# A gated recurrence with a low-rank mixer: transposes moved to ScalarE's DMA queue, one batch's input to the MLP formed as sums, and a new instruction order

## The chip, the cores and the metric

The kernel runs on one core of one Trainium2 chip. A core has a matmul engine (TensorE, PE), a vector engine (VectorE, DVE), an activation engine (ScalarE, ACT), a general engine (GpSimd, POOL) and a queue engine (SyncE, SP) that here only issues DMA transfers. The metric is device time in microseconds. The profile's span runs from the first to the last instruction of one profiled execution and is about 2 us shorter than the time.

## The reference

There are four batches of 768 tokens, eight heads of 48 channels (384 channels in all). First comes a linear recurrence with a gate per channel, then a low-rank mixing of tokens with a residual, then a two-layer MLP with a residual.

```python
for t in range(S):                                  # per batch and head
    state = alpha[t][:, None] * state + outer(k[t], v[t])
    y[t] = q[t] @ state
x = y                                               # (batch, 768, 384)
u = x + (x.T @ U @ V).T                             # U: 768x32, V: 32x768
out = u + relu(u @ w_ch1) @ w_ch2                   # 384 -> 1536 -> 384
```

## The kernel before, in words

**Tiles.** Tokens are cut into chunks of 128. Batches 0 and 1 (`PAIR`) are handled two tokens per partition and four heads at a time by `stage_pair`, batches 2 and 3 by `stage_gla`, one chunk and all eight heads at a time. Both do the same things: the logarithm of alpha on ACT (`lt`), one cumulative-sum matmul group on PE (`cb`, in `f_cum`), and three exponentials of it on ACT: `ai` (with minus), `aa`, and `tot`, the decay over a whole chunk. Then rk = k times ai and rq = q times aa on POOL or DVE; these two are transposed to kT and qT; scores are matmuls of kT with qT (`sc`), masked on DVE into `pm`; the state is carried from chunk to chunk by `db`, `sm` and `st`; and y comes from `pm`, rv (v in bf16) and the old state, and is copied into `xb`.

**The totals.** Two heads lie side by side on the 128 partitions, and the state needs their decays separately, with exact zeros for the other head. In `f_cum` a matmul of the identity with `offd` (8 columns holding 0 or -30000) is added to the sums, so that one exponential gives both the values and the zeros.

**The transposes.** A transpose is either a PE matmul group against the identity (L435 for pairs, L604 for `stage_gla`), whose result ACT or DVE copies out of PSUM, or a DMA transpose from SBUF to SBUF. The set `TRD` names the chunks whose kT and qT come by DMA: of batch 3, chunks 2 to 5. `TRU` names the batch, 3, whose u is transposed by DMA. Before, SyncE's queue issues them all (L595 and L735).

**The mixer.** `stage_mix` forms utx, the 32-row product of U and x. For a batch in `XT` (0 and 1) the transposed u is made on PE in one go: x is multiplied by the identity (L718) and the mixer's product is added to the same PSUM tile (L721); u itself is never formed, so `mlp2` adds the mixer's part once more at its end (L803). For the other batches the mixer's product (L730) is added to x on DVE, giving `ub`, and that is transposed, by PE (L746) for batch 2 or by DMA for batch 3.

**The MLP.** `mlp1` is 12 column groups by two halves of the tokens, three matmuls of 128x384 each (L773), whose results ACT or DVE pass through a maximum with zero into `h1t` (L783, L785). `mlp2` is 12 matmuls of 128x384 for each chunk (L798), then the residual add on DVE (L807) and the store (L808).

**The order.** Nothing runs in the order of the source. Each step is registered in `Plan` with its possible engines and a cost in nanoseconds. `TABLE` lists the steps' numbers in the order in which they are emitted, with a letter where the engine is chosen (A for ACT, V for DVE, G for POOL). `place` walks the table, picks buffers and keeps a clock for each engine; the clocks decide which buffer of a pool a step gets and how many dummy matmuls (`filler`) keep PE busy in the first 28 us. [...]

**Waits of transfers.** Every transfer, whichever queue issues it, takes one of eight semaphores in turn. It is issued only after the one that had the same semaphore, eight transfers earlier, has landed.

Of the kernel before, what the change touches and what calls it, by code (L numbers as in the profile page):

```python
# [8 lines left out]
FP32 = mybir.dt.float32  # L9
BF16 = mybir.dt.bfloat16  # L10
# [29 lines left out]
class Plan:  # L40
# [3 lines left out]
    BEGIN = {"DVE": 4400.0, "POOL": 3300.0, "ACT": 2900.0}  # L44
# [43 lines left out]
    def place(self, table):  # L88
# [6 lines left out]
        end = {}  # L95
        for x in table.split():
# [15 lines left out]
            if eng == "DVE" and op.port:  # L112
                t = max(t, port - self.PORT)
            op.t = t
            if eng == "SP" and op.mode == "X":
                dma = max(dma, t) + cost
                clock[eng] = t + cost
                end[op] = dma + 850.0
            elif eng == "SP":
                dma = max(dma, t + 600.0) + cost  # L120
                clock[eng] = max(t + 450.0, dma - 3500.0)
                end[op] = dma + 2000.0
            else:
                if eng == "PE" and op.mode != mode:
                    cost += self.SWITCH
                    mode = op.mode
                clock[eng] = end[op] = t + cost
                if eng == "POOL" or (eng == "DVE" and op.port):
                    port = end[op]
            for b in op.bufs:  # L130
                b.left -= 1
                b.last = max(b.last, end[op] + self.LAT[eng])
                if b.left == 0:
                    b.pool.free[b.idx] = b.last
# [19 lines left out]
67 65 69 179 61 182 201 184 157 77 62 63 183 66 204 160 205 187G 247 189 161 162 207 64 68 191V 164V 166 186V 188 190A 185 168V 165V 73 71 167 192 70  # L154
181G 180G 224 206 163 159G 169V 81 74 170 194 172 193 75 158G 209G 3 78 79 76 82 72 195 250 227 196 208V 83 173 211 210 251 228 268 229 197 213A 2 231G
171 174 80 271 175 198 212V 214 273 274 272 84 85 176 89 232V 233 253 252 234 215 254G 6 5 199 177 255G 4 226G 275G 203G 15 31 33 35 236V 23 13 17 93
19 21 27 29 235A 237 43 25 87 86 1 97 39 90 216 200A 238 256 257 230 225A 259A 258V 240 202A 178A 241 239 242 260 277 276V 243 244 217 249G 218 270G
219 88 95 278 37 41 262 261 51 47 49 91 279A 245 220 280A 222 248A 94 269G 8 281 7 57 59 45 55 221 388 263 283 53 101 96 32 34 16 36 264 18 14 24 20 92
284 285 98 105 391 410 394 246A 107 103 99 100 102 265 266 413 392 393 22 28 30 26 286 282 287 9 11 395G 0 267V 223V 288A 289 290 295 10V 12A 291A 414
292 304 298 299 293 296 300A 396G 301 417G 302 305 297A 307 308 294V 306V 303V 309A 415 332 330 328 352 354 331A 329A 432 416 336 355V 353A 435 356 438  # L160
357A 333V 344 312 340 320 314 345A 315A 313A 436 346 310 338 342 321V 455 337V 437 109 106 343V 112 104 108 113 316 398 334 318 347V 341V 335V 339V
311A 44A 40A 400A 390A 440G 38G 42G 348 458 397 419 326 322 317V 323V 349V 399A 327A 401 319A 461 389G 460 459 403 418V 421V 48G 439G 383 404 358 442
324 325A 50A 402 405 406 368 46G 420 350 412G 52A 444A 58A 441 411G 434G 433G 462G 407G 351V 422V 443A 363 364 359 56A 54A 60A 478 423 445 384 369 370
424 446 425 481 360 499 482 483 426 448 486G 447 361 371 449 502 385 365 505 450V 504 453 507G 427 386 428 366 509 464 488 485G 429G 511V 463V 110 362
111 129 367 457A 503 456A 490A 454A 408 471 378 409A 619 466A 451 506V 465 430 487 508 117 379 133 467V 472 123 116 121 114 118 115 473G 468 119 120
122 489V 130 125 431A 484 510A 479A 480A 500A 131 127 124 387 136 474 135 126 128 137 149 491 512 470 452V 493 492 469 373 494 380 475G 501A 638 621
374 495 640 515 623 622 496G 513 516 514 476 625 517V 375 497 627 381 629V 477A 626 620 642 641 376 718 498A 624 518 628 630V 720 519A 529 520 521 631
722 721 723 658 522V 535 523 526 633 833 527 538 539 524 530 528A 525V 660 536 532 533 531A 537V 634 662 540A 661 663 545 561 551 635 534V 587 559 644
664 645 639 585 588V 560A 581 546A 557 541 659 562A 643 569 567 632 553 570A 678 558A 542V 552V 554V 582A 372 134 666 575 680 145 573 681 682 574A 568A
683 586A 563 141 132 139 564A 668A 665 685 684 583 576V 584V 543 653 636 835 544A 646 837 647 547 555 649V 648A 637A 565 549 673 654 556V 548V 687 550A  # L170
836 667 144 377 655G 679 674 686 589 571 590 688V 566V 669V 572V 725 675G 724 838 698 689A 690 650 670 671 651 652 699 591 700 579 702 703 701 852 580V
592 692 705 704 609 656 594 595 727 693 577 691 657V 729A 672 694 578V 596 726 593 706 707 696 604 695V 597 697A 839 605 606 841 708A 709A 728A 713 714
614 843A 138 730 710 732 712 872 890 676 610 840 719 715G 854 731 677V 711 611 612 607 857 855 599 733 842 892 856 908 734A 844A 834 858 859 874 716
615 717V 845 875 893 735 600 861 877 142 143 598 613 153 140 147 148 154 895 736A 894 150 146 876 863A 926 847 846 751 745 743 860 749 616 744 746 752
853 878 750 739 740 848 601 879 753 747 737 850 849 617 862A 738 754A 864 151 155 867 928 741 851V 866 748A 783 910 781 782A 929 742V 784V 868 931 911
773 797 865 602 880 798A 777 779 799 800A 912 913 785 765 930 786V 778V 780V 766V 870 757 932 891 896 871V 881 898 761 795 791 771 775 758A 772A 796V
792V 787 873 897 915 933 914 869G 759 801 767 789 774A 768A 760A 776V 802V 885 899 917 763 769 788V 790V 886 916 887G 764A 770A 755 903 152 882 762V
909 900 918 756A 884 901 935 902 919 904 808 809 934 818 803 793 883 810 921 888 794A 156 905V 920 922 936 906 924 804 805 937 938 907A 923G 618 603
608 382 927 939 940A 889V 925V 806 813 941 942A 828 946 807 958 819 943 949 947 950 959 829 955 820 814 952 948 815 823 824 944 825 956 951 945 953 826
816 821 811 954 960 957 830 969 965 817 822 967 963 961 977 968A 966V 971 983 984A 964A 962V 981 972V 978V 985 1005 831 991 975 1014 973 976V 1009 970V  # L180
987 1006A 992V 974A 986A 988V 982V 1010 979 980A 832 995 989 990V 996A 1011 1007 993 999 1015 1016 1001 997 1012 1002V 994V 1000V 1017 1019 1003 1034
1013 1020 812 1018 1021 1022 1029 1024 998A 1008A 1004A 1025 1026 1035 1030 1036 1027 1023 1028 827 1031 1037 1038 1032 1033
# [8 lines left out]
def kernel(  # L191
# [33 lines left out]
    TRD = {(3, c) for c in range(2, NC)}  # L225
    TRU = (3,)
    XT = (0, 1)
# [633 lines left out]
```

## Time and profile before

| what | value |
|---|---|
| time, median of 3 | 165.16 us (165.06 to 165.35) |
| span of the profiled run | 162.8 us, TensorE clock 0.997 |
| q, k, u transposes by DMA | 14, each holds SyncE's queue for about 1.2 us |
| loads and weights | 24 tiles each of q, k, v, alpha and weights, 192 KB each |
| DMA engines | 30.43 MB moved, mean 187 GB/s |

The page gives for each engine the busy time and its share of the span, then the span in 40 slices of about 4 us, each with a digit for the busy tenth. Matmuls are pipelined: a matmul of 128x384 is shown with 326 ns, but a run of them starts one every 0.16 us. A row such as `L604 ... x4` in the timeline is a run of four, with the time at which it begins and its length.

### The profile page before, as it was taken

The numbers are of one execution on the slowest core, as the hardware profiler recorded it, in microseconds if no ns is written. First come the engines' busy times: TensorE is split into PE (matmuls) and PEld (weight loads), VectorE is DVE, ScalarE is ACT, GpSimd is POOL, SyncE is SP. The second block draws the span as 40 slices with busy tenths as digits, with TensorE's granted clock in tenths as the row PEclk, the third lists the DMA queues.
The fourth block names the chain that finished last, engine by engine and source line by source line (L and its number), as shares of the span: only waits on it lengthen the run. The fifth ranks groups of instructions, "written<-read, shape, count | busy, mean of one in ns | idle before, by whom it ended". The sixth has DMA issues, their size and how long they took to land.

```text
span 162.8 us, 4450 instructions
## 1 busy us (share of the span) xinstructions
PE 154.6 (95%) x1691; PEld 102.8 (63%) x1691; DVE 111.1 (68%) x240; ACT 87.9 (54%) x214; POOL 66.2 (41%) x106
## 2 busy tenths in 40 slices
PE   7878789999999999999999999999999999999991
PEld 2536677666666877766666766766667566666660
DVE  6389997536756989765579677896689465562512
ACT  4747787848594797956944557655432201330300
POOL 3228866659318625173685533519533000000000
PEclk9999999999999999999999999999999999999998
DMA  5999999999999999997998995995757133402124
GB/s 132 268 262 264 258 273 290 345 246 290 347 237 245 233 199 222 172 200 132 240 192 184 226 238 125 194 170 105 99 115 242 52 71 74 144 1 101 48 84 158
DMA packets 89876, 30.43 MB, mean 187 GB/s; under 512 B 83680, under 2 KB 89824, under 8 KB 89856
## 3 DMA queue, kind: packets, MB, share of 16 engines
q1 hardware_dynamic: 89856, 30.16, 81.7%
q8 instruction: 13, 0.21, 0.6%
q14 instruction: 7, 0.06, 0.1%
HBM read 23.79 MB, written 4.72 MB: 175 GB/s over the span
## 4 chain that ended last, share of the span: by engine, by line
PE 86%; DVE 6%; DMA 3%; SPq 2%; issue 1%
PE ps L798 29%; PE ps L773 29%; DMA io<-in_k_dram 3%; PE ps L435 3%; PE ps L543 2%; DVE pm L473 2%; SPq L356 2%; PE ps L604 2%; PE ps L625 2%; DVE rq L422 2%; PE ps L684 1%; PE ps L718 1%; PE ps L494 1%; PE ps L462 1%; PE ps L566 1%
## 5 line engine op out<-in xcount | busy, mean ns | idle before, releaser
L798 PE MATMUL ps<-w_sb,h1t 128*128 128x384 bf16 x288 | 54.2, 326 | 0.0
L773 PE MATMUL ps<-uT,w_sb 128*128 128x384 bf16 x288 | 50.9, 326 | 0.0
L783 ACT ACTIVATE h1t<-ps 128x384 bf16<-128x384 f32 x46 | 21.4, 496 | 35.4 <-PE ps L773 35.1
L785 DVE TENSOR_SCALAR h1t<-ps 128x384 bf16<-128x384 f32 x50 | 25.8, 552 | 21.0 <-PE ps L773 20.9
L773 PEld LDWEIGHTS <-w_sb 128*128 128x128 bf16 x288 | 27.3, 98 | 16.6
L798 PEld LDWEIGHTS <-h1t 128*128 128x128 bf16 x288 | 26.4, 97 | 16.4 <-issue 0.6
L635 DVE TENSOR_TENSOR pm<-ps,maskc 128x512 bf16<-128x512 f32 x24 | 15.6, 684 | 2.6 <-PE ps L625 2.5
L473 DVE TENSOR_TENSOR pm<-ps,maskp 128x512 bf16<-128x512 f32 x24 | 15.8, 682 | 1.3 <-PE ps L462 1.3
L584 POOL TENSOR_TENSOR rk<-io,ai 128x384 bf16<-128x384 f32 x12 | 11.0, 915 | 10.0 <-PE ps L773 3.9
L584 POOL TENSOR_TENSOR rq<-io,aa 128x384 bf16<-128x384 f32 x12 | 11.0, 927 | 2.2 <-ACT aa L578 1.2
L807 DVE TENSOR_TENSOR ou<-ub,ps 128x384 f32<-128x384 bf16 x12 | 6.4, 552 | 7.3 <-PE ps L798 7.1
L313 ACT CAST xb<-ps 128x384 bf16<-128x384 f32 x15 | 7.3, 491 | 7.0 <-PE ps L684 5.4
L317 POOL CAST rw<-io 64x384 bf16<-64x384 f32 x14 | 7.0, 503 | 8.0 <-DMA io<-in_v_dram 7.2
L317 POOL CAST rv<-io 128x384 bf16<-128x384 f32 x12 | 6.0, 503 | 9.6 <-DMA io<-in_v_dram 9.6
L317 POOL CAST w_sb<-io 128x384 bf16<-128x384 f32 x16 | 7.7, 507 | 4.7 <-DMA io<-in_moe_w_ch_dram 4.7
L313 ACT COPY kt<-ps 128x512 bf16<-128x512 bf16 x13 | 8.0, 612 | 2.5 <-PE ps L435 2.0
L313 ACT COPY qt<-ps 128x512 bf16<-128x512 bf16 x11 | 7.4, 677 | 3.3 <-PE ps L435 1.7
L315 DVE COPY qt<-ps 128x512 bf16<-128x512 bf16 x9 | 5.6, 627 | 4.6 <-PE ps L435 3.5
L659 POOL TENSOR_TENSOR st<-sm,tot 128x384 bf16<-128x384 f32 x6 | 5.0, 831 | 9.1 <-DVE sm L671 9.1
L422 POOL TENSOR_TENSOR rk<-io,ai 128x384 bf16<-128x384 f32 x8 | 7.3, 912 | 3.3 <-DMA io<-in_k_dram 1.4
L422 POOL TENSOR_TENSOR rq<-io,aa 128x384 bf16<-128x384 f32 x7 | 6.4, 913 | 5.3 <-ACT aa L416 5.3
L731 DVE TENSOR_TENSOR ub<-xb,ps 128x384 bf16<-128x384 bf16 x12 | 6.0, 550 | 3.3 <-PE ps L730 3.3
(120 smaller groups left out, 262.1 us busy)
## 6 DMA issues: line engine op xcount, KB each, us to landing
io<-in_q_dram SPq DMA_DIRECT2D x24, 192.0 KB, 4.4
io<-in_alpha_dram SPq DMA_DIRECT2D x24, 192.0 KB, 4.7
io<-in_k_dram SPq DMA_DIRECT2D x24, 192.0 KB, 4.7
io<-in_v_dram SPq DMA_DIRECT2D x24, 192.0 KB, 4.5
io<-in_moe_w_ch_dram SPq DMA_DIRECT2D x24, 192.0 KB, 4.4
out_dram<-ou SPq DMA_DIRECT2D x24, 192.0 KB, 2.2
v_in<-in_moe_V_dram SPq DMA_DIRECT2D x1, 96.0 KB, 4.4
u_in<-in_moe_U_dram SPq DMA_DIRECT2D x1, 96.0 KB, 4.0
```

The costliest lines, as they stand in the source:

```text
L313: nc.scalar.copy(dst, src)
L317: nc.gpsimd.tensor_copy(dst, src)
L422: eng.tensor_tensor(jh(dst()[:, :, 0:D]), raw(a), jh(x()), op=ALU.mult)
L473: nc.vector.tensor_tensor(dst, s2, maskp.to_broadcast([C, 2, 2, C]), op=ALU.mult)
L584: eng.tensor_tensor(dst()[:, :, 0:D], a(), x(), op=ALU.mult)
L635: nc.vector.tensor_tensor(pm()[:, :, par, :], s2, maskc.to_broadcast([C, HP, C]), op=ALU.mult)
L731: P.add({"DVE": 465}, lambda e, c=c, hb=hb: nc.vector.tensor_tensor(ub()[:, c, :], xb()[:, c, :], hb()[:, 0:DM], op=ALU.add), r=[hb] + xk( ...
L773: nc.tensor.matmul(hb()[:, 0:TW], lhsT=w1_sb[:, ct, jt * 128 : (jt + 1) * 128], rhs=uT()[:, ct, tt * TW : (tt + 1) * TW], start=(ct == 0), ...
L783: nc.scalar.activation(dst, hb()[:, 0:TW], AF.Relu)
L785: nc.vector.tensor_scalar_max(dst, hb()[:, 0:TW], 0.0)
L798: nc.tensor.matmul(hb()[:, 0:DM], lhsT=h1()[:, jt, c * C : (c + 1) * C], rhs=w2_sb[:, jt, :], start=(jt == 0), stop=(jt == NJ - 1 and not ...
L807: P.add({"DVE": 468}, lambda e: nc.vector.tensor_tensor(ou(), (xb if b in XT else ub)()[:, c, :], hb()[:, 0:DM], op=ALU.add), r=[hb] + (xk ...
```

## The change

There are five parts.

1. `TRD` now holds all six chunks of batch 3, so chunks 0 and 1 also get kT and qT by DMA; and all DMA transposes are issued by ScalarE's queue and no longer by SyncE's. It takes PE work away and keeps SyncE's queue free for loads and stores.
2. `XT` is now batch 0 alone: batch 1's u is formed as a sum on DVE and transposed by PE, so that its `mlp2` needs no extra matmul.
3. For batches 1 to 3 the matmul with `offd` is dropped. Two exponentials with a bias of 0 or -30000 for each partition (`offb`) write the even and the odd entries of `tot`.
4. The last chunk of the last batch is computed and stored as 256 and 128 columns, so that less work follows the last matmul.
5. The planner gets a model of the wait for the eighth transfer back, other costs for transfers, and more choices of engine (`u_sb`, the w1 casts, rv, rk and rq); `TABLE` is a new one throughout.

```diff
-    TRD = {(3, c) for c in range(2, NC)}
+    TRD = {(3, c) for c in range(NC)}
-    XT = (0, 1)
+    XT = (0,)
...
+            queued = eng == "SP" or op.mode == "X"
+            if queued and len(lanes) >= 8:
+                t = max(t, lanes[-8])
...
-            nc.tensor.matmul(cb()[:, DM : DM + 2 * HP], lhsT=ident, rhs=offd.rearrange("p a b -> p (a b)"), start=False, stop=False)
             for p in range(HP):
                 nc.tensor.matmul(
-                    cb()[:, DM + 2 * p : DM + 2 * p + 2],
+                    cb()[:, DM + p : DM + p + 1],
                     lhsT=lt()[:, 2 * p : 2 * p + 2, :].rearrange("t h w -> t (h w)"),
                     rhs=ones, start=False, stop=(p == HP - 1),
...
-        P.add({"ACT": 100}, lambda e: nc.scalar.activation(tot()[:, :, 0], cb()[:, DM : DM + 2 * HP], AF.Exp), r=[cb], w=[tot])
+        def f_tot(e):
+            for i in range(2):
+                nc.scalar.activation(tot()[:, i : 2 * HP : 2, 0], cb()[:, DM : DM + HP], AF.Exp, bias=offb[:, i : i + 1])
+        P.add({"ACT": 200}, f_tot, r=[cb], w=[tot])
...
-                    {"SP": 1250.0},
-                    lambda e, ring=ring, dst=dst: nc.sync.dma_start(dst(), ring().rearrange("t h w -> t (h w)"), transpose=True),
+                    {"ACT": 1250.0},
+                    lambda e, ring=ring, dst=dst: queue(e).dma_start(dst(), ring().rearrange("t h w -> t (h w)"), transpose=True),
...
-                    {"SP": 1250.0},
-                    lambda e, c=c: nc.sync.dma_start(uT()[:, :, c * C : (c + 1) * C], ub()[:, c, :], transpose=True),
+                    {"ACT": 1250.0},
+                    lambda e, c=c: queue(e).dma_start(uT()[:, :, c * C : (c + 1) * C], ub()[:, c, :], transpose=True),
...
+        parts = [(0, 256), (256, DM)] if b == B - 1 and c == NC - 1 else [(0, DM)]
```

`queue(e)` is ScalarE's or SyncE's DMA queue by the engine chosen. In the pair stage the total sums are dropped to four columns in the same way for batch 1, while batch 0 keeps the old form.

## The prediction

> **What bounds the kernel now.** I read the busy table first, then the slices, the chain of waits, the stretches in the middle, and last the timeline of the places that the change touches. From the page:
>
> ```profile
> PE 154.6 (95%) x1691; PEld 102.8 (63%) x1691; DVE 111.1 (68%) x240; ACT 87.9 (54%) x214; POOL 66.2 (41%) x106
> PE   7878789999999999999999999999999999999991
> DVE  6389997536756989765579677896689465562512
> ACT  4747787848594797956944557655432201330300
> PE 86%; DVE 6%; DMA 3%; SPq 2%; issue 1%
> ```
>
> A busy PE can still be waiting, so I took the start-to-start times. In the timeline a run of n equal matmuls lasts n-1 steps and one pipeline depth. Five of 128x384 take 0.97 us with 0.326 each, so a step is (0.97-0.33)/4 = 0.16 us; four of 128x128 take 0.39 with 0.22 each, a step of 0.056. The 8-column matmul moves the next start by about 0.028 (from 76.16 to 76.18 here, 68.64 to 68.67 elsewhere).
>
> ```profile
> 75.28 0.39 PE L604 MATMUL ps<-ident,rk 128*128 128x128 bf16 x4
> 75.50 0.65 PE L773 MATMUL ps<-uT,w_sb 128*128 128x384 bf16 x3
> 75.99 0.33 PE L566 MATMUL ps<-lt,tri 128*128 128x384 bf16 x1
> 76.16 0.17 PE L567 MATMUL ps<-offd,ident 128*128 128x8 bf16 x1
> 76.18 0.24 PE L569 MATMUL ps<-ones,lt 128*128 128x2 bf16 x4
> 76.28 0.97 PE L773 MATMUL ps<-uT,w_sb 128*128 128x384 bf16 x5
> ```
>
> Over the whole trace the starts follow one another at these steps from about 27 us to 159.2 us. What exceeds them there is almost all at changes of the array's tiling: a trip to the narrow score matmuls and back costs about 0.30 us (0.096 + 0.061 + 0.146 around the one at 84 us). So PE is the bound for 132 of 162.8 us, and a microsecond of PE work is a microsecond of time, as long as the others keep feeding it. Do they? Now the stretches of batches 2 and 3; the columns are the stretch, its length, busy PE, PEld, DVE, ACT, POOL, the granted clock, the DMA share and GB/s:
>
> ```profile
> 90.00:100.00 10.00, 10.00 (x143) 7.23 (x142) 6.83 (x14) 6.12 (x15) 4.85 (x7) 1.00 0.91 197
> 100.00:110.00 10.00, 10.00 (x116) 6.66 (x114) 8.94 (x18) 6.09 (x16) 2.78 (x4) 1.00 1.05 183
> 110.00:120.00 10.00, 10.00 (x98) 6.49 (x96) 6.58 (x14) 5.25 (x13) 7.25 (x10) 1.00 0.58 95
> ```
>
> ACT has four of ten microseconds free there. That is the room into which the change puts the transposes, which SyncE's queue issues now:
>
> ```profile
> 106.19 2.09 SPq L363 DMA_DIRECT2D io<-in_q_dram  x1
> 108.39 1.52 SPq L595 DMA_TRANSPOSE kt<-rk  x1
> 110.01 1.19 SPq L595 DMA_TRANSPOSE qt<-rq  x1
> 116.91 1.53 SPq L363 DMA_DIRECT2D io<-in_v_dram  x1
> ```
>
> A transpose holds its issuing queue for 1.2 us and lands 2.4 us after the issue began (median; 3.9 at most). The end:
>
> ```profile
> 157.52 2.93 SPq L808 DMA_DIRECT2D out_dram<-ou  x4
> 158.89 1.20 DVE L807 TENSOR_TENSOR ou<-ub,ps 128x384 f32<-128x384 bf16 x2 [1.40 <-PE ps L798]
> ```
>
> The last matmul ends at 159.5; a full-width add of 0.55 and a 192 KB store follow it.
>
> [...] The trace shows no biased one; its unbiased tot exponentials take 190 ns. [...] equal-sized loads on SyncE's queue are shown with 0.38 to 2.1 us; no run here shows an issue from ScalarE. [...]
>
> **The change on PE.** (a) Eighteen of the 24 ident-times-offd matmuls go (L404 for batch 1, L567 for 2 and 3): 18 x 0.028 = 0.50 us. The narrower right-hand sides of the total sums save nothing: 25 ns a step already at two columns. (b) Batch 1 leaves XT. The six L721, the six L803 and 18 identity matmuls L718 go; six L730 and 18 transposes L746 come. The 18s cancel at 0.056 each; six of 384 columns remain saved: 6 x 0.1625 = 0.98 us. (c) Chunks 0 and 1 of batch 3 lose their PE transposes: 16 x 0.056 = 0.90 us. (d) The last chunk is done as 256 and 128 columns: twelve times (0.109 + 0.056 - 0.1625), +0.03 us. (e) The instruction order of the changed program has 20 score trips where the old has 19 (its neighbours were merged differently): +0.30 us. Sum: 0.50 + 0.98 + 0.90 - 0.03 - 0.30 = 2.05 us less PE work.
>
> **The end.** The last add is 128 columns wide. From 0.55 us for 384, with about 1.04 ns a column, it falls to about 0.28; the store is 64 KB and not 192 KB, which at the 260 GB/s of the first slices is up to 0.5 us less, of which I count a third. Its 256-column half is added and issued during the twelve matmuls before. Together -0.4 us (bounds 0.2 and 0.8).
>
> **The start.** The first mlp1 matmul is at 29.36 us. Until then DVE is busy nearly without a gap from 7.9 us. In the new order DVE does before it three products with k, two kt and one qt less, and one product with q, one vm_sb and the utx copy more: about 1.5 us less. But the first product it does now waits for the seventh load (the sixth and the eighth landed around 9 us in the old trace), about 0.8 us later, and the 23rd load, near 20.5 us, still feeds the last q. Three cumulative-sum groups of batch 1 are done before mlp1 instead of two (0.4 us of PE work brought forward). I put the start at nothing, bounds -0.8 and +0.8.
>
> **ScalarE.** It loses 4 transposed copies or so to the DMA and gets 18 transposes, 36 biased exponentials for 18 plain ones, and some weight casts. To see where, I laid the instruction orders of both programs along a ruler of PE work (the steps above). Between 89.5 and 106.7 on it, 17.2 us, ScalarE has 10 transposes (10 x 1.2 = 12.0), 5 wide exponentials (x 0.37, the step of the pair at 6.70 us), 8 h1t evictions (x 0.38), one cast (0.4) and 6 biased exponentials (x 0.19[...]): 12.0 + 1.9 + 3.0 + 0.4 + 1.1 = 18.4 us. That is 1.2 us more than PE gives it. In the old order the ruler's stretch from 80 to 110 held 42 ACT instructions, some 19 us of 30. Queued behind the transposes are h1t evictions, whose PSUM banks PE wants back, and the ai and aa for the chunks that follow. The transposes wait for the POOL and DVE products rk and rq, and for the eighth transfer back. The last one stands 3.85 us of ruler before the scores that read it and needs 2.4 to land, so 1.4 us are spare: the 1.2 of overload just fits, if a transpose costs ScalarE what it costs SyncE. I take 0.5 us of PE stall in this stretch, bounds 0 and 4. The six u transposes of batch 3 come later, where ScalarE was busy for 0.49 of 10 us (130 to 140), and have the same distance to their reader as before; no cost.
>
> **Hidden at nothing.** Batch 1's six ub adds on DVE (6 x 0.55) replace six uT evictions of like length; three evictions of 0.5 to 0.8 come, beside some 10 us of mlp2 matmuls of batch 0. SyncE is freed: its loads and stores no longer stand behind transposes waiting for rk; POOL waits of 9.6 us for v were off the chain already. The extra memsets run before the first load lands.
>
> **Forecast.** 165.16 - 2.05 - 0.4 + 0 + 0.5 = 163.2 us.
>
> **Rivals.** *ScalarE's queue becomes the bound* (0.15). SyncE's loads and ScalarE's transposes go out at the same time, and loads are shown with up to 2.1 us. If each transpose takes 0.4 us more on ScalarE, ten of them need 4.0 more: 1.2 + 4.0 - 1.4 = 3.8 us of PE stall instead of 0.5, so 163.2 + 3.3 = 166.5. For it: the page's DMA row is full until 73 us and near full to 110. Against: six of eight kt and qt issues took 1.19 to 1.22 with loads in flight. This one ends slower. *The saving is given back in small stalls* (0.08): DVE in the same stretch has 33 instructions, about 16.6 of 17.2 us, so both evicting engines are full and each late bank costs PE a little; at 1.7 us more it is 164.9, no change. *The start gains* (0.09): if DVE's 1.5 us count in full and the transposes are free, 163.2 - 0.7 - 0.5 = 162.0. Against: the loads set the pace there. The forecast's own case keeps 0.68.
>
> **How the numbers follow.** Faster: the forecast and the last rival, 0.77, and a little of the second, 0.78. Same 0.06, slower 0.16. The range: at the low end all the favourable bounds, 165.16 - 2.05 - 0.8 - 0.6 = 161.7; at the high end I go into the first rival, to 166.0, leaving about one in ten above.
>
> **What would show it.** Right: starts of matmuls that follow at the old steps through 90 to 125 us; no L404 kind for batch 1; PE's last matmul near 157.3 us; an add of about 0.28 us at the end; DMA_TRANSPOSE rows on ACT's queue with 1.2 us. Wrong: gaps between matmuls at 95 to 115 us released by ACT (h1t, kt, qt), transposes of 1.5 us and more on ACT, or a first mlp1 matmul that is over 1 us away from 29.4.

## The result, and the profile after

The changed kernel takes 164.47 us (median of 4, 164.14 to 164.77) where the kernel before, in the same runs, takes 165.11 (164.97 to 165.35). The ratio is 0.9959, 95% interval 0.9936 to 0.9983: 0.64 us less. The forecast was 163.2 us, 1.96 less. The direction was right and the size was not; the prediction failed in what it took for the transposes.

About half of the 0.64 us lies outside the profile's span. Time less span is 2.06 to 2.19 us in every execution of the kernel before, and 1.74 to 1.85 us in the four of the changed kernel. Of the runs below, the ten whose kernel has the tile `offb` show the smaller difference (1.73 to 1.99 us), before_memset too, which has nothing of the change but that tile and its memsets; before_act and before_fetch, without it, show the larger. What makes it is open.

First the page of the changed kernel: the busy row, the slices of PE and ACT, and the chain of waits by engine and by line.

```profile
PE 152.9 (94%) x1662; PEld 101.4 (62%) x1663; DVE 117.4 (72%) x255; ACT 92.4 (57%) x232; POOL 60.5 (37%) x94
PE   7879989999999999999999999997989995999992
ACT  4798999758798766736977464553353100453000
PE 74%; DMA 11%; ACT 7%; DVE 2%; issue 2%; POOL 1%; SPq 1%; DVEq 0%; ACTq 0%
PE ps L831 25%; PE ps L801 25%; DMA qt<-rq 6%; DMA uT<-ub 3%; DMA io<-in_alpha_dram 2%; PE ps L653 2%; PE ps L459 2%; PE ps L632 2%; PE ps L567 2%; PE ps L518 2%; ACT ai L431 1%; PE ps L486 1%; PE ps L712 1%; PE ps L758 1%; PE ps L590 1%
```

Before, PE's row was all nines from the seventh slice to the last but one, and DMA had 3% of the chain. Now there are three dents late in the row, and 11% of the chain is DMA: two of the transposed tiles, `qt<-rq` and `uT<-ub`, stand in it. ScalarE's 7% all lies before 23 us. Next the stretches (stretch, length, busy PE, PEld, DVE, ACT, POOL, granted clock, DMA share, GB/s) and, from the timeline of PE, the runs that had to wait:

```profile
110.00:120.00 10.00, 9.10 (x101) 5.93 (x100) 8.77 (x18) 3.86 (x10) 3.03 (x6) 1.00 1.17 211
120.00:130.00 10.00, 9.47 (x106) 5.81 (x104) 5.63 (x12) 3.04 (x7) 0.83 (x1) 1.00 0.01 1
130.00:140.00 10.00, 8.33 (x53) 4.83 (x51) 4.52 (x10) 0.49 (x1) 0.00 (x0) 1.00 0.86 178
```

```profile
112.45 0.85 PE L653 MATMUL ps<-qt,kt 48*128 48x128 bf16 x24 [0.90 <-DMA qt<-rq]
...
121.85 0.40 PE L653 MATMUL ps<-qt,kt 48*128 48x128 bf16 x8 [0.53 <-DMA qt<-rq]
...
136.41 1.78 PE L801 MATMUL ps<-uT,w_sb 128*128 128x384 bf16 x10 [1.67 <-DMA uT<-ub]
```

The brackets give idle time and its releaser: each of the three ends with the landing of a transpose. They show 0.90, 0.53 and 1.67 us, 3.1 together; from start to start, compared with the same places of after_head below, where PE does not wait, the three cost 1.0 + 0.7 + 1.8 = 3.5 us, because idle time is counted from a matmul's shown end, and a matmul of 128x384 is shown with 0.33 us where the next of a run starts 0.16 us after it. Behind all three lies this. The last rows of the DMA list give the median time from issue to landing (the arrival of the data), first of the kernel before, then of the changed one:

```profile
uT<-ub SPq DMA_TRANSPOSE x6, 2.4
kt<-rk SPq DMA_TRANSPOSE x4, 2.8
qt<-rq SPq DMA_TRANSPOSE x4, 2.4
```

```profile
qt<-rq ACTq DMA_TRANSPOSE x6, 5.0
kt<-rk ACTq DMA_TRANSPOSE x6, 4.0
uT<-ub ACTq DMA_TRANSPOSE x6, 3.8
```

The end came out as forecast. In the changed kernel's timeline:

```profile
159.43 0.42 DVE L843 TENSOR_TENSOR ou<-ub,ps 128x256 f32<-128x256 bf16 x1 [0.81 <-PE ps L831]
160.11 0.29 DVE L843 TENSOR_TENSOR ou<-ub,ps 128x128 f32<-128x128 bf16 x1 [0.26 <-PE ps L831]
```

From the start of the last matmul to the end of the span it is 3.20 us where it was 3.66.

The two profiled executions add up like this (us):

| part | before | after | difference |
|---|---|---|---|
| start, to the first mlp1 matmul | 29.36 | 28.45 | -0.9 |
| from there to the last matmul's start, without the three waits | 129.8 | 127.8 | -2.0 |
| the three waits for transposes | 0 | 3.5 | +3.5 |
| from the last matmul's start to the end | 3.66 | 3.20 | -0.5 |
| span | 162.8 | 163.0 | +0.1 |
| outside the span | 2.1 | 1.8 | -0.3 |
| time of this execution | 164.95 | 164.77 | -0.2 |

The profiled execution of the changed kernel is the longest of its four; its median is 0.3 us shorter.

### The profile page after: what moved, and what is told of

The parts are those of the page before. It is cut to its first block, busy times and chain, and to the rows that moved or that the text cites. A ratio compares the mean times of both kernels' runs of the same rounds, so it can differ in the third digit from the quotient of the medians.

```text
span 163.0 us, 4417 instructions
## 1 busy us (share of the span) xinstructions
PE 152.9 (94%) x1662; PEld 101.4 (62%) x1663; DVE 117.4 (72%) x255; ACT 92.4 (57%) x232; POOL 60.5 (37%) x94
## 4 chain that ended last, share of the span: by engine, by line
PE 74%; DMA 11%; ACT 7%; DVE 2%; issue 2%; POOL 1%; SPq 1%; DVEq 0%; ACTq 0%
PE ps L831 25%; PE ps L801 25%; DMA qt<-rq 6%; DMA uT<-ub 3%; DMA io<-in_alpha_dram 2%; PE ps L653 2%; PE ps L459 2%; PE ps L632 2%; PE ps L567 2%; PE ps L518 2%; ACT ai L431 1%; PE ps L486 1%; PE ps L712 1%; PE ps L758 1%; PE ps L590 1%
## 5 line engine op out<-in xcount | busy, mean ns | idle before, releaser
L831 PE MATMUL ps<-w_sb,h1t 128*128 128x384 bf16 (+2 forms) x300 | 53.7, 319 | 0.0
L843 DVE TENSOR_TENSOR ou<-ub,ps 128x384 f32<-128x384 bf16 (+2 forms) x19 | 9.7, 528 | 11.4 <-PE ps L831 11.3
L612 POOL TENSOR_TENSOR rq<-io,aa 128x384 bf16<-128x384 f32 x9 | 8.5, 947 | 9.4 <-ACT aa L601 6.2
L759 DVE TENSOR_TENSOR ub<-xb,ps 128x384 bf16<-128x384 bf16 x18 | 8.8, 547 | 4.2 <-PE ps L758 4.2
L324 ACT COPY qt<-ps 128x512 bf16<-128x512 bf16 x14 | 9.6, 688 | 2.0 <-PE ps L632 1.1
L600 ACT ACTIVATE ai<-ps 128x384 bf16<-128x384 f32 x12 | 5.9, 500 | 5.0 <-PE ps L592 4.2
L601 ACT ACTIVATE aa<-ps 128x384 bf16<-128x384 f32 x12 | 5.8, 497 | 3.8 <-DVE ub L759 1.7
L446 DVE TENSOR_TENSOR rq<-io,aa 128x384 bf16<-128x384 f32 x7 | 5.4, 771 | 3.4 <-DMA io<-in_q_dram 3.4
L328 POOL CAST w_sb<-io 128x384 bf16<-128x384 f32 x11 | 5.6, 505 | 5.5 <-DMA io<-in_moe_w_ch_dram 5.3
L400 ACT ACTIVATE lt<-io 128x384 bf16<-128x384 f32 x12 | 6.1, 525 | 2.1 <-DMA io<-in_alpha_dram 2.1
```

The lines of the kernel that those rows point to most:

```text
L324: nc.scalar.copy(dst, src)
L328: nc.gpsimd.tensor_copy(dst, src)
L446: eng.tensor_tensor(jh(dst()[:, :, 0:D]), raw(a), jh(x()), op=ALU.mult)
L612: eng.tensor_tensor(dst()[:, :, 0:D], a(), x(), op=ALU.mult)
L759: P.add({"DVE": 465}, lambda e, c=c, hb=hb: nc.vector.tensor_tensor(ub()[:, c, :], xb()[:, c, :], hb()[:, 0:DM], op=ALU.add), r=[hb] + xk( ...
L831: nc.tensor.matmul(hb()[:, 0 : hi - lo], lhsT=h1()[:, jt, c * C : (c + 1) * C], rhs=w2_sb[:, jt, lo:hi], start=(jt == 0), stop=(jt == NJ - ...
```

## The experiments

Two questions: why do the transposes land late, and where does the start's 0.9 us come from? The theories for the first: ScalarE or its queue is overloaded (the prediction's); the loads on SyncE's queue take the DMA engines' time; or a fetch of PE's own instructions does. The last came from the trace. The page's DMA queues list "q8 instruction: 13, 0.21", thirteen packets of 16 KB. In the changed kernel they lie at 106.6, 119.7 and 132.3 us in this stretch, one for every 106 to 145 matmuls (each of which has a weight load). That they are PE's is read from this count, and from the runs below, in which more matmuls near the start bring them earlier (the fetch of 106.6 us comes at 104.0 in after_shift, with 28 more). The DMA answer for 132 to 134 us, in 40 slices of 0.05 us:

```profile
DMA  9999199900000001001001001200290200100000
GB/s 297 184 189 215 56 82 394 36 0 0 0 0 0 0 0 36 5 31 36 5 31 36 5 31 36 36 31 10 51 15 0 31 0 0 31 0 0 0 31 31
q8 instruction: 1, 0.02, 2.9%
uT<-ub ACTq DMA_TRANSPOSE x2, 4.4
```

The fetch is the 394 in the seventh slice. Right behind it the traffic falls to 0 to 51 GB/s while transposes and stores are in flight: sixteen packets, fifteen of SyncE's queue (q1) and one of ScalarE's (q10), stay open for up to 2.5 us. The first of the sixteen had started 0.4 us before the fetch. At 107.0 us it is 22 packets and about 1.4 us. Meanwhile a few others go on, mostly up to four in each 0.1 us. Why these packets stay open is not shown: the records do not name a packet's engine. At 119.7 us nothing is held open: the transpose was nearly done, and its last two packets start at 120.6 us, when the fetch ends.

Not every fetch does this. In the 14 traces 36 such fetches overlap a transpose between its issue and its landing; twelve of them leave 11 to 25 packets open for more than 0.8 us. Of the 146 others after the first 10 us none leaves more than one. Shorter holds, 16 to 20 packets for 0.6 to 0.8 us, come without any fetch too, where loads run beside a transpose (before_act at 110.4 us, after_oneexp at 100.3, after_sync at 105.6).

All times are medians; that of the kernel before was 165.0 us (164.97 to 165.05) beside every one of them.

| run | time, us | ratio to before, 95% |
|---|---|---|
| after_sync | 166.78 | 1.0109 (1.0077 to 1.0140) |
| before_act | 168.89 | 1.0221 (1.0188 to 1.0254) |
| after_shift | 162.55 | 0.9839 (0.9810 to 0.9868) |
| before_fetch | 165.72 | 1.0042 (1.0025 to 1.0059) |
| after_warm | 162.44 | 0.9869 (0.9823 to 0.9915) |
| after_light | 162.82 | 0.9860 (0.9815 to 0.9906) |
| after_head | 162.10 | 0.9830 (0.9803 to 0.9856) |
| after_best | 163.56 | 0.9906 (0.9877 to 0.9934) |
| after_oneexp | 163.30 | 0.9882 (0.9843 to 0.9922) |
| before_bias | 163.49 | 0.9905 (0.9889 to 0.9921) |
| before_gla | 163.60 | 0.9908 (0.9882 to 0.9934) |
| before_memset | 163.75 | 0.9927 (0.9903 to 0.9951) |

**after_sync and before_act: the queue exchanged.** In the changed kernel both kinds of transpose, qT and kT in one line and uT in another, go back to SyncE's queue; in the kernel before both go to ScalarE's. The line for uT:

```diff
-lambda e, c=c: queue(e).dma_start(uT()[:, :, c * C : (c + 1) * C], ub()[:, c, :], transpose=True),      # after_sync
+lambda e, c=c: nc.sync.dma_start(uT()[:, :, c * C : (c + 1) * C], ub()[:, c, :], transpose=True),
...
-lambda e, c=c: nc.sync.dma_start(uT()[:, :, c * C : (c + 1) * C], ub()[:, c, :], transpose=True),       # before_act
+lambda e, c=c: nc.scalar.dma_start(uT()[:, :, c * C : (c + 1) * C], ub()[:, c, :], transpose=True),
```

> The changed kernel with its 18 DMA transposes issued by SyncE's queue again, at the same places of the order. Landing theory (a transpose from ScalarE's queue shares the 16 DMA engines with the loads and stores that SyncE issues meanwhile, so it lands 4 to 6 us after its issue and not 2.4, and PE waits for it at 111, 121 and 134 us): landing falls to about 2.4 to 3 us, two or three of the three PE waits (3.5 us in all) go, and the time falls by 1 to 3 us from 164.5, unless loads held up behind the transposes make a new wait. ScalarE theory (the transposes overload ScalarE): the waits go as well, and ScalarE's h1t evictions come earlier. Fetch theory (a 16 KB instruction fetch in the middle of transposes stops all transfers for 1 to 2.4 us, whichever queue issued them): the wait before the last mlp1 stays at about 1 to 2 us.

> The kernel before with its 14 transposes issued by ScalarE's queue, nothing else changed. Landing theory: the eight q and k transposes land after 3.5 to 6 us in place of 2.4 to 3.9, since loads and stores now run beside them; the old order has 5 to 9 us between a transpose and its reader, so the time stays within 0.3 us of 165.1, or loses up to 1 us at u. ScalarE theory: each transpose keeps ScalarE's later instructions from running for 1.2 us; rows of ACTIVATE would not overlap rows of DMA_TRANSPOSE. Against it: in the changed kernel they do overlap.

Both are slower, and neither for the expected reason. On SyncE's queue, with this order, transposes and loads stand behind one another: the transposes go out later (the last `uT` at 140.7 us and not 135.7), PE still waits (1.7 us at 111.5, 1.2 at 122.6, 1.4 at 141.5, and 1.1 at 126.7 for GpSimd's `st`), and some landings still take 3.3 to 5.5 us. So the late landings don't belong to ScalarE's queue alone.

before_act gives the landing theory its cleanest test, since nothing but the queue differs. The first three transposes of q and k, at 108 to 112 us, now have loads beside them and land in 4.70, 4.04 and 4.13 us; on SyncE's queue, where loads stood in order with them, they took 3.08, 2.41 and 2.48. No fetch falls on them. The other five, without loads, land in 2.4 to 2.5 us, and five of the six of u in 2.3 to 2.4 (the last in 3.4). So ScalarE's queue by itself is no slower, and loads beside a transpose cost it about 1.6 us.

That is not what made before_act slow. In its order, which was not made for it, ScalarE's evictions stand behind transposes that are not ready. Its timeline, ACT and then PE:

```profile
118.50 1.23 ACTq L595 DMA_TRANSPOSE qt<-rq  x1
119.83 1.23 ACTq L595 DMA_TRANSPOSE kt<-rk  x1
121.11 0.49 ACT L783 ACTIVATE h1t<-ps 128x384 bf16<-128x384 f32 x1 [3.10 <-DMA qt<-rq]
```

```profile
121.65 0.38 PE L625 MATMUL ps<-qt,kt 48*128 48x128 bf16 x7 [1.68 <-ACT h1t L783]
```

That is the rival of the prediction, an eviction behind a transpose and PE behind the eviction, and it exists; but in before_act, not in the changed kernel, where no such wait is left on PE after the start. The wait is only part of the 3.9 us, too. The granted clock (the column before the last two) fell after it, and eight steps of 128x384 matmuls took up to 0.32 us and not 0.16, 1.2 us more in all:

```profile
122.00:124.00 2.00, 1.67 (x13) 0.92 (x13) 1.97 (x4) 0.36 (x1) 0.00 (x0) 0.50 0.46 94
124.00:126.00 2.00, 2.00 (x10) 0.96 (x8) 2.00 (x4) 0.00 (x0) 0.00 (x0) 0.65 0.19 38
```

Five of its six executions show a mean clock of 0.988 to 0.990 and take 168.7 to 169.4 us; the sixth, with 0.998, takes 167.3. In the changed kernel the clock stayed at 1.00 through its waits. There the transposes fit among the ACTIVATEs:

```profile
97.50 1.21 ACTq L623 DMA_TRANSPOSE kt<-rk  x1
97.75 0.42 ACT L605 ACTIVATE tot<-ps,offb 128x4 f32<-128x4 f32 x2
98.04 0.51 ACT L601 ACTIVATE aa<-ps 128x384 bf16<-128x384 f32 x1
98.41 0.52 ACT L600 ACTIVATE ai<-ps 128x384 bf16<-128x384 f32 x1
98.78 0.55 ACT L324 CAST rv<-io 128x384 bf16<-128x384 f32 x1
99.18 0.54 ACT L600 ACTIVATE ai<-ps 128x384 bf16<-128x384 f32 x1
```

The issue runs from 97.50 to 98.71 us. The rows from `tot` to `rv` stand ahead of the transpose in `TABLE`: the issue began while they were still to be executed. The `ai` of 99.18 us is the first behind it. So it is for all 18 transposes: the next instruction behind starts 0.05 us or more after the end of the issue.

**after_shift, before_fetch and after_warm: the instruction fetch moved.** Dummy matmuls near the start are split into more and smaller ones, which changes the place of all later fetches and nothing else of the later work.

```diff
+        if 9 < len(made) <= 13:                  # after_shift; before_fetch: if len(made) <= 12
+            for _ in range(8):
+                nc.tensor.matmul(ps[:, 7, 0:1], lhsT=filler[:, 0:128], rhs=filler[:, 0:1], start=True, stop=True)
+        else:
+            nc.tensor.matmul(ps[:, 7, :], lhsT=filler[:, 0:128], rhs=filler, start=True, stop=True)
...
+        for n in (440, 1, 1) if len(made) <= 14 else (512,):     # after_warm
+            nc.tensor.matmul(ps[:, 7, 0:n], lhsT=filler[:, 0:128], rhs=filler[:, 0:n], start=True, stop=True)
```

> The changed kernel with four of the dummy matmuls near 8 us replaced by 32 of one column, which take about the same time and put 56 more instructions into PE's stream. Fetch theory: each fetch of PE's instructions comes 56 instructions earlier, the one at 132.3 us near 128, ahead of the u transposes; no packet of more than 2 us stands there, u lands in order after 2.4 to 4 us each, and the PE wait of 1.8 us before the last mlp1 shrinks to under 0.5: the time falls by 1.0 to 1.8 us. Landing theory alone: the wait stays as it is, and the time stays within 0.3 us of 164.5.

> The kernel before, where the six u transposes (130 to 139 us, SyncE's queue, nothing else moving) land in 2.3 to 2.4 us. Twelve fillers at the start become eight one-column matmuls each, 84 matmuls more, so that the fetch of PE instructions that came at 147.4 us comes near 132 to 135 us. Fetch theory: the u transposes in flight then land in 3.5 to 5 us, those before and after in 2.3 to 2.4; their readers come 3.5 down to 2 us after the landing now, so PE waits 0 to 1.0 us; time 165.0 to 166.0 us. Rival (the late landings of the changed kernel belong to ScalarE's queue, or to the stores beside them): all six stay at 2.3 to 2.4 us, time 165.0 us.

> The changed kernel with the same 28 matmuls more ahead as in the earlier shift (162.55 us), placed so that PE stays busy: each of 14 fillers becomes one of 440 columns and two of 1. Fetch theory: fetches again near 104, 117.5 and 127, so the waits at 121 and 134 us are gone and that at 111 us stays; with no loss of granted clock at the start, first mlp1 matmul at 28.4 to 28.9, time about 162.3 us (161.8 to 162.8). If it was the one-column matmuls, and not the place of the fetches, that brought the earlier gain: about 164.4 us.

after_shift and after_warm both gain 1.9 to 2.0 us over the changed kernel with 28 matmuls more. (That eight one-column matmuls take about as long as one of 512 was the author's estimate, from the prediction's step of 0.025 us and the fillers' of 0.21; their own step is not shown.) The waits at 121 and 134 us are gone in both; the one at 111 us stays (1.4 us in after_shift, 0.6 in after_warm; the fetch lies at 104.0 and 103.9). before_fetch has no wait, as the readers of the transposes concerned have time to spare there, but the landings follow the fetches in both directions. Each line is one transpose and its counterpart:

| transpose, issued at | fetch at | landing, us | counterpart without a fetch near it | landing, us |
|---|---|---|---|---|
| after: uT 130.0 | 132.3 | 5.89 | after_shift: uT 130.2 | 4.12 |
| after: uT 131.4 | 132.3 | 4.92 | after_shift: uT 131.5 | 3.09 |
| after: qt 117.6 | 119.7 | 4.07 | after_shift: qt 118.5 | 2.50 |
| before: kt 115.7 | 116.9 | 3.86 | before_fetch: kt 116.2 | 2.43 |
| before_fetch: kt 120.0 | 121.2 | 3.73 | before: kt 119.8 | 2.44 |
| before_fetch: uT 135.4 | 136.5 | 3.46 | before: uT 135.2 | 2.40 |
| before_fetch: uT 136.7 | 136.5 | 3.02 | before: uT 136.5 | 2.38 |

So in these pairs a transpose with a fetch near it lands 0.6 to 1.8 us later, on SyncE's queue as on ScalarE's. before_fetch's own 0.7 us more is not explained by this: its profiled span is only 0.2 us longer, and that is its later start; but the profiled execution, 165.13 us, is the fastest of its 22.

**after_light, after_head and after_best: what is left at 111 us.** In the first two, batch 3's later loads bring four heads, or one, of eight, and leave out the rest of its data; in the third, three mlp1 groups are put ahead of the three score groups.

```diff
-    nc.sync.dma_start(t(), src[b, :, sl, :].rearrange("h t d -> t h d"))
+    hs = slice(0, 4 if b == 3 and t.idx in full else H)        # after_light, on after_shift; after_head: 1, on after_warm
+    nc.sync.dma_start(t()[:, hs, :], src[b, hs, sl, :].rearrange("h t d -> t h d"))
...
-... 877 895 859 896 878 879 897 766 762 927V 860 798 767A 763A 880 ...      # TABLE, after_best, on after_shift
+... 766 762 798 767A 763A 799A 877 895 859 896 878 879 897 927V 860 880 ...
```

> Base: the changed kernel with 56 PE instructions more ahead (162.55 us, with one wait of 1.44 us at 111.7 us left, for the transposed qt that took 5.97 us to land). Here batch 3's loads from about 97 us on carry half the heads each (4 of 8), so the output of batch 3 is not the reference's; nothing else differs. Theory A (the transposes land late because the loads on SyncE's queue share the 16 DMA engines with them): the kt and qt transposes issued from 97 to 108 us land in 2.4 to 3.5 us instead of 3.9 to 6.4, the wait at 111.7 us shrinks below 0.3 us, time about 161.2 us. Theory B (a transpose issued by ScalarE lands late whatever else moves): landings of 4 to 6 us as before, wait of 1.4 us stays, time about 162.5 us.

> The version with 14 fillers of 440, 1 and 1 columns; of batch 3, loads from about 97 us on bring one head of eight each, so batch 3's output is not the reference's. With half of the heads the transposes still landed in 3.5 to 5.3 us, though the wait at 111.7 us went. Theory A (the loads beside them on the 16 DMA engines): with an eighth of the packets the transposes of 102 to 108 us land in 2.4 to 3.0 us unless a fetch falls on them; no wait at 111 us; time about 1.4 us below the version with full loads. Theory B (a transpose from ScalarE's queue lands late by itself, or behind others of its own queue): 4 to 6 us still.

> Same base (162.55 us). Only the written order differs: the nine mlp1 matmuls (three groups) that stood behind the three score groups of batch 3 at 111.7 us now stand ahead of them, with their evictions. If that wait is a lack of 1.4 us between transpose and reader: nine matmuls are 9 x 0.163 = 1.5 us, the wait shrinks to under 0.2 us, time about 161.2 us. If what follows the scores (mask products, the outputs) is just as short of time, the wait comes back at the next reader: 162.5 us.

With half of the loads the landings hardly moved (3.5 to 5.3 us), but the last one before the scores landed in 3.53 instead of 5.97, and the wait at 111 us was gone. With an eighth they came down for good. The DMA list of after_head, and the timeline of PE:

```profile
qt<-rq ACTq DMA_TRANSPOSE x6, 2.6
kt<-rk ACTq DMA_TRANSPOSE x6, 3.7
uT<-ub ACTq DMA_TRANSPOSE x6, 3.1
```

```profile
109.83 2.28 PE L815 MATMUL ps<-uT,w_sb 128*128 128x384 bf16 x13
112.04 0.84 PE L667 MATMUL ps<-qt,kt 48*128 48x128 bf16 x24
```

The score group follows without a bracket. Those of 104.6, 106.0 and 107.4 us land in 2.7 to 3.3; the two kt beside a fetch (102.1 and 114.1, with fetches at 102.6 and 116.1) take 3.8 and 4.0. That fits theory A; in the median, though, the loads are worth 0.3 us and not 1.4. The time of after_warm varies from one execution to the next (161.9 to 164.2 us), that of after_head hardly (161.9 to 162.5); that it is the remaining wait which varies is likely, not shown.

Fewer loads moved something else as well. A second queue of instruction fetches, q14, brings 8 KB at a time. In the changed kernel one falls at 110.3 us, while the last `qt` before the scores is in flight, and behind it the traffic stands at 5 to 15 GB/s for 0.6 us (DMA answer for 110 to 112 us):

```profile
GB/s 196 219 224 224 208 380 200 220 210 230 200 200 220 215 184 223 205 88 5 15 10 10 5 10 10 10 10 10 10 10 54 261 250 273 253 269 250 273 253 269
q14 instruction: 1, 0.01, 1.7%
```

after_shift, after_warm and after_oneexp, which wait at 111 us, have it at 109.4, 109.6 and 109.0 us, with packets held open for 0.7 to 0.8 us; in after_light and after_head it lies at 104.6 and 102.9 us and holds none. No run moves it alone, and holds of that length come without a fetch as well, so how the wait at 111 us divides between the loads and this fetch stays open.

after_best did what it should at one place and gained nothing. The wait for `qt` is gone, but against the same steps of after_shift four small ones come at 115.2 to 121.8 us (0.33, 0.35, 0.23 and 0.18 us), the first two for `pm`, the masked scores: what follows the scores has no time to spare either. It and after_light also start 0.5 us later than after_shift. In their profiled executions the granted clock was 0.83 from 10 to 20 us, where one-column matmuls stand in for full ones; that of after_shift escaped it (1.00), and after_warm, with 440 columns kept, had 1.00 throughout.

**after_oneexp: ScalarE relieved.** On after_warm; the kernel leaves out the bias, and with it the zeros for the other head.

```diff
-            for i in range(2):
-                nc.scalar.activation(tot()[:, i : 2 * HP : 2, 0], cb()[:, DM : DM + HP], AF.Exp, bias=offb[:, i : i + 1])
+            src = cb()[:, DM : DM + HP].rearrange("p (h o) -> p h o", o=1).to_broadcast([128, HP, 2])
+            nc.scalar.activation(tot()[:, :, 0].rearrange("p (h o) -> p h o", o=2), src, AF.Exp)
```

> The same version with full loads; each pair of biased exponentials becomes one without bias that writes both columns, so the decays of batches 1 to 3 do not start afresh in the other half and those outputs are not the reference's. ScalarE loses 18 ACTIVATEs of 0.19 us net, 3.4 us, of which some 0.6 lie in the stretch from 97 to 107 us. Step of the prediction (an overload of ScalarE's queue delays PE there): time 0.5 us or more below the full version. If ScalarE has room and the waits are landings: within 0.3 us of the full version, the wait at 111 us as long.

163.30 us, against 162.44 of after_warm: not faster. Its profiled execution waits 1.4 us for `qt` at 111 us. In the changed kernel the second exponential of a pair starts 0.146 us after the first (median of 18 pairs), so what was taken from ScalarE is about 2.6 us by estimate, 18 x 0.146, and not 3.4. So these exponentials are not what PE waits for, which speaks against an overload of ScalarE.

**before_bias, before_gla and before_memset: the start.** Part 3 of the change put into the kernel before (before_bias); then for batches 2 and 3 only (before_gla); then nothing of it but its memsets (before_memset).

```diff
-            nc.tensor.matmul(cb()[:, DM : DM + 2 * HP], lhsT=ident, rhs=offd.rearrange("p a b -> p (a b)"), start=False, stop=False)
+            for i in range(2):
+                nc.scalar.activation(tot()[:, i : 2 * HP : 2, 0], cb()[:, DM : DM + HP], AF.Exp, bias=offb[:, i : i + 1])
...
+    offb = const.tile([C, 2], FP32, name="offb")                  # in before_memset these lines alone
+    nc.vector.memset(offb, 0.0)
+    nc.vector.memset(offb[0:64, 1:2], -30000.0)
+    nc.vector.memset(offb[64:128, 0:1], -30000.0)
```

> The kernel before with part 3 alone: biased exponentials for batches 1 to 3, 18 matmuls with offd fewer. If PE work counts one for one, 18 x 0.028 = 0.50 us less than 165.1. If ScalarE's 36 exponentials of 0.19 us each (about 3.5 us more than before) held anything up, the time would not fall.

> The kernel before with the biased exponentials in batches 2 and 3 alone: 12 of the 18 identity-times-offd matmuls go, batches 0 and 1 are computed as before. If part three is worth its PE work alone: 12 x 0.028 = 0.34 us, first mlp1 matmul at 29.3 to 29.4 us, time about 164.7 us. If the 1.1 us that the start gained in the version with all of part three comes from the start's small shifts (the extra memsets, two products of VectorE that no longer meet one of GpSimd), and not from batch 1's exponentials, it comes here too: first mlp1 near 28.3 us, time about 163.6 us.

> The kernel before with four small memsets more on VectorE ahead of everything (the tile offb, which nothing reads); no instruction else differs. In the kernel before, two of VectorE's products with q overlap one of GpSimd and take 1.26 and 0.89 us where such a product takes 0.55 elsewhere (1.04 us too much, on an engine that the first mlp1 matmul waits for). If the start of the versions with biased exponentials was early because those overlaps fell away with a small shift in time: it can happen here too, first mlp1 matmul at 28.3 to 28.7 us, both products under 0.75 us, and time about 164.1 us. If the start gain belongs to something else in those versions: first mlp1 matmul at 29.3 to 29.4, time 165.0 us.

before_bias gained 1.5 us and not 0.5, before_gla 1.45 and not 0.34, and three memsets (not four, as expected there) of a tile that nothing reads gained 1.24 us by themselves. The first mlp1 matmul comes at 28.25, 28.54 and 27.95 us instead of 29.36. The matmuls that went are worth what the prediction said: from the first mlp1 matmul on, sixteen steps of before_bias add up to 0.45 us less and the twelve of before_gla to 0.33, 0.028 each; small new waits of 0.11 to 0.15 us give part of it back. The rest is the start, and the timelines show how. DVE and then POOL of the kernel before:

```profile
16.27 1.26 DVE L422 TENSOR_TENSOR rq<-io,aa 128x384 bf16<-128x384 f32 x1
...
21.14 0.89 DVE L422 TENSOR_TENSOR rq<-io,aa 128x384 bf16<-128x384 f32 x1
```

```profile
16.21 0.91 POOL L422 TENSOR_TENSOR rk<-io,ai 128x384 bf16<-128x384 f32 x1 [0.56 <-DVE kt L315]
...
21.11 0.50 POOL L317 CAST rw<-io 64x384 bf16<-64x384 f32 x1 [0.21 <-DMA io<-in_v_dram]
```

and DVE of before_memset:

```profile
15.77 0.55 DVE L426 TENSOR_TENSOR rq<-io,aa 128x384 bf16<-128x384 f32 x1
...
19.93 0.57 DVE L426 TENSOR_TENSOR rq<-io,aa 128x384 bf16<-128x384 f32 x1
```

In the kernel before, each of the two products starts 0.03 to 0.06 us after an operation of GpSimd and ends 0.41 and 0.42 us after that one's end (17.53 against 17.12, 22.03 against 21.61). With half a microsecond of shift they meet nothing and take 0.55 and 0.57. The other products `rk` and `rq` on VectorE show the same in the traces of the kernel before and of the changed one: the twelve (these two among them) that start with 0.18 us or more of a GpSimd operation still to run end 0.41 to 0.42 us after that operation and take 0.60 to 1.26 us; the twelve that start with none of one, or with up to 0.12 us, take 0.54 to 0.56. What holds them is not shown. It costs 0.71 + 0.32 = 1.0 us here, on an engine that is busy without a gap from 11 to 27 us. before_act, which has no memsets more, meets both again (1.21 and 0.88 us); before_bias and before_gla do not (0.55 to 0.73). The rest of before_memset's earlier start, about 0.4 us, was there before 16 us: its first logarithms start 0.2 to 0.3 us earlier, with the landing of their loads. Why they land earlier is not shown; no run has the tile without its memsets.

## Why the prediction was wrong

- **PE bounds the kernel and its work falls by 2.05 us: right.** From the first mlp1 matmul to the last the steps add up to 2.0 us less without the three waits. About 0.4 us of one cumulative-sum group moved to the time before, so 2.4 were to be expected there. Taken at its usual length (the lower quartile of its kind in four of these traces), every step together gives 2.36 us less; the missing 0.4 are small waits of up to 0.17 us, as at 61.1, 61.8 and 63.1 us.
- **The end, -0.4: right.** It measured -0.46, with an add of 0.29 us for 128 columns against the 0.28 forecast.
- **The step that failed: "needs 2.4 to land, so 1.4 us are spare".** It took the landing time from transposes that mostly ran with few loads beside them, and put it where most of the twelve of q and k run beside batch 3's loads, the six of u beside stores, and three instruction fetches fall among them. There most took 4 to 6 us. The distances were near the 3.85 us of the working or above: the last `qt` was issued 3.5 us ahead of the place where PE could have read it and landed after 4.1 (a wait of 0.7), the one issued at 106.6 us had 4.9 us and landed after 5.7 (a wait of 1.0). The stall was put at 0.5 us; it measured 3.5. Moving the fetches gives 2.0 us of it back, thinning out the loads as well another 0.3, in medians. That a transpose on ScalarE's queue lands later with SyncE's loads beside it is what before_act shows (4.0 to 4.7 us in place of 2.4 to 3.1); the working counted a second queue for the time of its issues and not for the landings. The prediction's 0.5 us for an overload of ScalarE has no counterpart: PE nowhere waits for ScalarE there, and after_oneexp took such work away and gained nothing. The 0.19 us for a biased exponential in that overload was the author's estimate; the second of a pair starts 0.15 us after the first.
- **"The same distance to their reader as before; no cost" for the u transposes: the distance held, the cost did not.** From the issue of the third, the last that the first reader needs, to that reader it is 3.3 us before and would have been 3.2 now. But it landed after 4.9 us, and the largest wait, 1.8 us, is there. A fetch at 132.3 us fell on it; in after_shift and after_warm, where the fetches come earlier, the wait is gone.
- **The start, at nothing: 0.9 us too pessimistic, 1.3 with the cumulative-sum group.** The measured gain lies just beyond the bound of -0.8 (which the low end of the range counted as 0.6). How much of it is the planned lesser work of DVE and how much the accident of GpSimd's and VectorE's products was not separated for the changed kernel; its own products of that kind take 0.56 to 0.94 us there. before_memset shows that the accident alone can be worth as much.
- **The rivals.** ScalarE's queue as the bound: not in this order, though before_act shows the mechanism in another. The saving given back, 164.9 us, was nearest in time, by luck; the cause named there, small stalls for late banks, was not the one. The start's gain came, but not the free transposes that its 162.0 us stood on.

So the gain that the change was made for was there, and the waits took it back: 164.95 - 0.9 - 2.0 + 3.5 - 0.5 is 165.05 us, and the 0.3 us outside the span make it 164.75, against 164.77 for the profiled execution. What is left of the gain in that execution is of the size of this last, unexplained part.

## What to carry to other kernels

Give each transfer the landing time that it has among its neighbours (4.0 to 4.7 us for a transpose beside loads here), not its time alone (2.4), and look on the DMA queues for traffic that the program never issued. This kernel, bound by one engine and ordered by hand, is decided at the level of a microsecond by coincidences: before a small gain is credited to an edit, run the same kernel with a dead instruction in its place (three dead memsets were worth 1.24 us here). Where it is a fetch that collides, some cheap instructions elsewhere move it: 28 matmuls more near the start brought the one of 106.6 us to 104.0.

## What the runs showed of the hardware

- Of 36 fetches of 16 KB of PE's instructions that overlapped a DMA transpose (14 traces), twelve left 11 to 25 DMA packets open for more than 0.8 us, for 1.3 to 2.5 us at the longest; of 146 others none left more than one. Beside a fetch a transpose landed 0.6 to 1.8 us later. Behind 8 KB fetches of q14 14 to 26 packets stayed open for 0.7 to 0.8 us in five of 14 cases; holds of 0.6 to 0.8 us came three times without a fetch.
- A transpose from SBUF to SBUF lands in 2.3 to 2.4 us alone, whether SyncE or ScalarE issues it, in 4.0 to 4.7 us beside loads of 192 KB (before_act), in 5.9 us where a fetch falls on it as well (`kt` of 104.7 us in the changed kernel, fetch at 106.6), and in up to 6.7 in after_warm.
- The issue of a transpose by ScalarE, 1.2 us, starts while ACTIVATEs ahead of it in the order are still to run; those behind it start 0.05 us or more after its end.
- A biased exponential of 128x4 took 265 to 275 ns on average where the unbiased one of 128x8 took 180 to 190; the second of a biased pair starts 0.15 us after the first.
- The three memsets were worth 1.24 us, about 0.3 of it outside the span: twice the measured effect of the whole change.
